# Four plain pairs instead of two ahead of the seven-product pairs, all sums off GpSimd, the last two pairs side by side

## The chip, the cores and the metric

The kernel runs on one core of a Trainium2 chip. The metric is device time in microseconds (us), the median of some runs. TensorE is called PE (its weight loads PEld), VectorE DVE, ScalarE ACT, GpSimd POOL and SyncE SP, as in the profile.

## The reference

Causal attention over 2 batches, 12 heads, 448 positions and 64 features per head, followed by two residual blocks on x of shape 2 x 448 x 768. The weights are 768 x 3072 and 3072 x 768.

```python
x = attention(q, k, v)
xn = (x - mean(x)) / sqrt(var(x) + 1e-6) * g_ln          # block 1
x = x + maximum(xn @ w_ch1, 0) @ w_ch2
x = x + real(fft(fft(x, axis=1), axis=2))                 # block 2
un = (x - mean(x)) / sqrt(var(x) + 1e-6)
x = x + maximum(un @ w2_ch1, 0) @ w2_ch2
```

## The kernel before, in words

x is held as tiles `x[b, j]` of 128 features x 448 positions (batch b of 2, feature tile j of 6). Every large product is made of three matmuls (`mm3`, L98 to L100): a float32 operand is split into a high part (ACT copy, L94) and a low part (a DVE subtraction, L95), and low x high, high x low and high x high are added in PSUM. So one product of a 128 x 128 weight tile with 448 columns is three matmuls.

A block's 3072 hidden features are 24 tiles m, taken as 12 pairs c of two. A **plain pair** (`ff1`) makes its 2 tiles for both batches from 6 feature tiles each: 2 x 2 x 6 x 3 = 72 matmuls. A **seven-product pair** (`ff1_pair`) uses the seven-product scheme for 2 x 2 blocks (the blocks are batches, halves of the features and the two tiles m): P1 to P7, each 3 tiles x 3 matmuls, 63 in all. It needs sums of the operands: on the x side `combine` makes S1 to S4 once a block (12 subtractions or additions, L716, on POOL; their splits are `xs`, L94 and L95), on the weight side every pair needs four subtractions of 128x384 (L225, on POOL but for the first pair of a block, which takes DVE). The second product of a pair (`ff2`: `ff2_sum`, then the addition onto x by DVE, L688) is 6 matmuls for each (b, j), 12 of them.

Weights come packed over SP's queue (`w_load`, 96 loads) and are unpacked by ACT (L173) and DVE (L176, `wf`), then split (`wsp`). `w_steps` is a generator that goes through the list `plan`; `w_tick` takes one step of it wherever it stands among the other instructions, and at most six `wsp` slots are held at a time. A scheduler then sets each engine's final order by what is ready and by place in the program; each engine executes its own list in order.

One block: `ff_lead` makes the hidden tiles 0 to 3 of batch 0, while the mean and the centred tiles of batch 1 are made. `ff_middle` makes tiles 0 to 3 of batch 1; meanwhile ACT and DVE make the squares (`sq`, L520, L524), PE sums them (`lnv`, L529), ACT takes the root (`sd`, L552), POOL spreads it on a diagonal (`sdiag`, L554) and PE turns that into rows (`rps`, L562), which ACT stores as `std` (L564). x is multiplied by `std` (L684: DVE for batch 0, POOL for batch 1) before the first addition. Then come the second products of the two plain pairs, ten seven-product pairs (each with the second products of the pair before as fills between its first three products), and at the end `ff2_last`: for the first three j of the order both last pairs in one PSUM sum (12 matmuls), for the other three the last pair alone (6), then the addition and a multiplication by 1/std (`rstd`, L690).

Between the blocks stands the Fourier step: `fold` adds and subtracts halves of x (`even`, `odd`, L804, L805, on POOL), folds them by position (L795 ACT, L796 and L798 DVE) and splits the result (`eo`); `stage1` multiplies with cosines and sines into `abps` (386 columns), `stage2` (`mixps`) adds to x, and `ln_sum` adds up the tiles for the next mean (`lnacc`, L494, POOL but for the last) which PE turns into `lnm` (L508). `FIRST_LAST` is the order in which `ff2_last` and `fold` take the tiles.

Of the kernel before, what the change touches and what calls it, by code (L numbers as in the profile page):

```python
# [43 lines left out]
PLAIN = 2  # L44
# [10 lines left out]
def fused_kernel(ctx: ExitStack, tc: tile.TileContext, aps, out):  # L55
# [87 lines left out]
    for moe in range(2):  # L143
        plan += [("w", moe, 1, m) for m in range(PLAIN * NM)]
        plan += [("w", moe, 2, u) for u in range(PLAIN * 2)]
        plan += [("pair", moe, c) for c in range(PLAIN, NCH)]
        plan += [("w", moe, 2, 2 * NCH - 2 + u) for u in range(2)]
# [41 lines left out]
    def w_whole(unit):  # L189
        f = decoded()  # L190
        yield True
        t = yield from w_slot(unit, 2 if unit[2] == 1 else 6)
        split(t[:, 0], t[:, 1], f, nc.gpsimd if unit[1:3] == (1, 1) else None)
        w_ready[unit] = t
        yield True

    def w_between(unit, u):
        _, moe, c = unit
        if c > PLAIN:
            yield from w_whole(("w", moe, 2, 2 * c - 2 + u))  # L200
        else:
            yield True
            yield True

    def w_steps():
        for unit in plan:
# [3 lines left out]
            half = COLS // 2  # L210
            f = decoded()
            b11, b21 = f[:, :half], f[:, half:]
            yield True
            t = yield from w_slot((unit, 0), 2)
            split(t[:, 0], t[:, 1], f)
            w_ready[unit, "P1"], w_ready[unit, "P2"] = (t, 0), (t, 3)
            yield True
            f2 = decoded()
            b12, b22 = f2[:, :half], f2[:, half:]
            yield True  # L220
            t = phalf.tile([P, 2, half], F32R, tag="h", name="wsh")
            split(t[:, 0], t[:, 1], b22)
            w_ready[unit, "P3"] = (t, 0)
            e = nc.vector if unit[2] == PLAIN else nc.gpsimd
            sub = lambda out, a, b: e.tensor_tensor(out=out, in0=a, in1=b, op=ALU.subtract)  # L225
            sub(b11, b12, b11)
            sub(b12, b22, b12)
            sub(b22, b22, b11)
            sub(b21, b21, b22)
            yield True  # L230
            yield from w_between(unit, 0)
            t = yield from w_slot((unit, 1), 2)
            split(t[:, 0], t[:, 1], f2)
            w_ready[unit, "P7"], w_ready[unit, "P6"] = (t, 0), (t, 3)
            yield True
            yield from w_between(unit, 1)
            t = yield from w_slot((unit, 2), 2)
            split(t[:, 0], t[:, 1], f)
            w_ready[unit, "P5"], w_ready[unit, "P4"] = (t, 0), (t, 3)
            yield True  # L240
# [244 lines left out]
    def ln_sum(b, j, src=x):  # L485
# [7 lines left out]
        e = nc.vector if src is xa or n_acc[b] == NJ else nc.gpsimd  # L493
        e.tensor_tensor(out=ln_acc[b], in0=acc, in1=src[b, j], op=ALU.add)  # L494
# [3 lines left out]
    def ln_rest(b, g):  # L498
# [51 lines left out]
        def deviation():  # L550
# [51 lines left out]
    def ff1_pair(moe, c, fills, after):  # L602
# [27 lines left out]
        def fill():  # L630
            for _ in range(after):
                if fills:
                    w_tick()
                    fills.pop(0)()

        kept("p1", product("P1", "a", True))
        w_tick()
        fill()
        kept("u2", product("P6", "a", False))
        w_tick()  # L640
        fill()
        kept("p7", product("P7", "b", True))
        w_tick()
        fill()
        o = product("P5", "a", False)
        added("p7", o, 1, m + 1)
        w_tick()
        o = product("P2", "c", True)
        added("p1", o, 0, m)
        w_tick()  # L650
        for name in ("P3", "P4") if c == NCH - 1 else ("P4", "P3"):
            if name == "P4":
                o = product("P4", "b", False)
                added("u2", o, 1, m)
            else:
                relu_split(0, m + 1, product("P3", "a", False))
            w_tick()
# [24 lines left out]
    def scale_x(j, b):  # L682
        e = nc.gpsimd if b else nc.vector
# [419 lines left out]
```

## Time and profile before

| what | us |
|---|---|
| median of 3 runs (855.33 to 860.99) | 855.5 |
| the profiled execution | 855.13 |
| its span, first to last instruction | 853.4 |
| PE busy | 819.7 |
| DVE busy | 661.2 |
| ACT busy | 415.4 |
| POOL busy | 238.1 |

Matmuls overlap in the pipeline: one lasts about 0.37 us in the trace and the next starts 0.20 us after it, so PE's time is read from starts, or from the number of matmuls in a stretch, not from the sum of durations. The attention ends at about 107 us; block 1 is from there to 455.6, the Fourier step to about 510 and block 2 to the end.

### The profile page before, as it was taken

To read this page: it belongs to the slowest core of one execution; us is meant where nothing else is said; L and a number is where in the kernel's file an instruction comes from. 1 tells how busy PE (TensorE), PEld (TensorE's weight loads), DVE (VectorE), ACT (ScalarE), POOL (GpSimd) and SP (SyncE) were. 2 spreads that over 40 slices of the span, in tenths; PEclk is the share of its full clock that TensorE was granted. 3 is DMA by queue.
4 is the path that set the end of the run, shared out by engine and by line. 5 is a ranking of instruction groups with operands and counts; after the bars stand their busy time and mean duration, and the time that the engine had idled before them with its cause. 6 is when DMAs were issued, how large, how long until landed. Compare 5 with 4: busy or idle time off the path is not lost. (4 is left out here: it accounts for less than half of the span.)

```text
span 853.4 us, 11883 instructions
## 1 busy us (share of the span) xinstructions
PE 819.7 (96%) x4484; PEld 730.6 (86%) x4484; DVE 661.2 (77%) x1097; ACT 415.4 (49%) x763; POOL 238.1 (28%) x230
## 2 busy tenths in 40 slices
PE   6999897999999999999997899799999999999997
PEld 5777686888999999999996779698999999999997
DVE  5778888999886777867679769999877786777744
ACT  6899997355444344433542335435444444344310
POOL 5433009422220222112057326632112220222002
PEclk9999999899999999999999799899999999999999
DMA  8431424135334224333463300113343333223003
GB/s 316 136 102 28 156 75 147 38 109 181 118 116 143 88 102 143 112 115 109 148 226 120 111 1 15 60 59 130 107 149 111 112 118 141 89 99 109 1 1 129
DMA packets 21433, 93.29 MB, mean 109 GB/s; under 512 B 2768, under 2 KB 4568, under 8 KB 21376
## 3 DMA queue, kind: packets, MB, share of 16 engines
q1 hardware_dynamic: 19152, 86.68, 30.0%
q0 software_dynamic: 2080, 5.62, 2.1%
q8 instruction: 35, 0.57, 0.3%
q14 instruction: 22, 0.18, 0.1%
q10 hardware_dynamic: 144, 0.23, 0.1%
HBM read 88.40 MB, written 2.75 MB: 107 GB/s over the span
## 5 line engine op out<-in xcount | busy, mean ns | idle before, releaser
L688 DVE TENSOR_TENSOR x<-x,yps 128x448 f32<-128x448 f32 x276 | 164.8, 613 | 100.5 <-PE yps L100 100.3
L98 PE MATMUL yps<-h,wsp 128*128 128x448 f32 x576 | 212.2, 369 | 0.8 <-ACT h L578 0.5
L99 PE MATMUL yps<-h,wsp 128*128 128x448 f32 x576 | 211.3, 367 | 0.1
L100 PE MATMUL yps<-h,wsp 128*128 128x448 f32 x576 | 210.7, 366 | 0.0
L225 POOL TENSOR_TENSOR wf<-wf 128x384 f32<-128x384 f32 x72 | 92.8, 1289 | 367.7 <-DVE wsp L95 329.4
L173 ACT ACTIVATE top<-wraw 128x768 f16<-128x768 bf16 x96 | 104.5, 1089 | 146.6 <-DVE wf L176 101.6
L95 DVE TENSOR_TENSOR wsp<-wf,wsp 128x768 fp32r<-128x768 f32 x112 | 109.4, 977 | 28.1 <-ACT wsp L94 27.8
L94 ACT ACTIVATE wsp<-wf 128x768 fp32r<-128x768 f32 x116 | 96.9, 836 | 55.3 <-PE yps L100 45.2
L176 DVE SCALAR_TENSOR_TENSOR wf<-wraw,top 128x768 uint32<-128x768 uint32 x96 | 112.6, 1172 | 9.7 <-ACT top L173 7.2
L98 PEld LDWEIGHTS yps<-h,wsp 128*128 128x128 f32 x576 | 108.5, 189 | 11.9 <-DVE x L688 1.4
L99 PEld LDWEIGHTS yps<-h,wsp 128*128 128x128 f32 x576 | 108.6, 188 | 10.1 <-issue 0.8
L100 PEld LDWEIGHTS yps<-h,wsp 128*128 128x128 f32 x576 | 108.5, 188 | 8.9 <-issue 0.2
L98 PE MATMUL hps<-xn,wsp 128*128 128x448 f32 x276 | 102.0, 370 | 0.0
L100 PE MATMUL hps<-xn,wsp 128*128 128x448 f32 x276 | 101.6, 368 | 0.0
L99 PE MATMUL hps<-xn,wsp 128*128 128x448 f32 x276 | 101.6, 368 | 0.0
L98 PE MATMUL hps<-xs,wsp 128*128 128x448 f32 x180 | 65.8, 366 | 0.0
L99 PE MATMUL hps<-xs,wsp 128*128 128x448 f32 x180 | 65.8, 365 | 0.0
L100 PE MATMUL hps<-xs,wsp 128*128 128x448 f32 x180 | 65.7, 365 | 0.0
L623 ACT ACTIVATE kept<-hps 128x448 f32<-128x448 f32 x60 | 32.3, 538 | 57.9 <-PE hps L100 57.9
L578 ACT ACTIVATE h<-kept 128x448 fp32r<-128x448 f32 x60 | 34.4, 574 | 49.0 <-DVE kept L627 48.9
L100 PEld LDWEIGHTS hps<-xn,wsp 128*128 128x128 f32 x276 | 52.2, 189 | 4.6 <-issue 0.4
L98 PEld LDWEIGHTS hps<-xn,wsp 128*128 128x128 f32 x276 | 52.3, 189 | 4.5 <-issue 0.4
(149 smaller groups left out, 1238.8 us busy)
## 6 DMA issues: line engine op xcount, KB each, us to landing
wraw<-in_w SPq DMA_DIRECT2D x96, 768.0 KB, 4.3
qkv<-in_qk SPq DMA_DIRECT2D x11, 448.0 KB, 3.5
qkv<-in_v SPq DMA_DIRECT2D x12, 256.0 KB, 4.7
out_t<-x SPq DMA_DIRECT2D x12, 224.0 KB, 1.9
x<-xr POOLq DMA_DIRECT2D x6, 222.2 KB, 2.9
cd<-in_cd POOLq DMA_DIRECT2D x3, 386.0 KB, 4.8
sd<-in_sd POOLq DMA_DIRECT2D x3, 386.0 KB, 8.1
cs<-in_cs POOLq DMA_DIRECT2D x2, 448.0 KB, 3.8
```

Source lines behind the costliest of these rows:

```text
L94: nc.scalar.activation(out=hi, in_=src, func=ACTF.Copy)
L95: (engine or nc.vector).tensor_tensor(out=lo, in0=src, in1=f32(hi), op=ALU.subtract)
L98: nc.tensor.matmul(out=dst, lhsT=w_lo, rhs=x_hi, start=first, stop=False, **kw)
L99: nc.tensor.matmul(out=dst, lhsT=w_hi, rhs=x_lo, start=False, stop=False, **kw)
L100: nc.tensor.matmul(out=dst, lhsT=w_hi, rhs=x_hi, start=False, stop=last, **kw)
L173: nc.scalar.activation(out=top_t.bitcast(F16)[:, 1::2], in_=raw.bitcast(BF16)[:, 4::4], func=ACTF.Copy)
L176: nc.vector.scalar_tensor_tensor(out=f.bitcast(U32), in0=raw.bitcast(U32)[:, 1::2], scalar=13, in1=top_t, op0=ALU.logical_shift_right, op1 ...
L225: sub = lambda out, a, b: e.tensor_tensor(out=out, in0=a, in1=b, op=ALU.subtract)
L578: nc.scalar.activation(out=t[:, 0], in_=src, func=ACTF.Relu)
L623: nc.scalar.activation(out=sums[name], in_=src, func=ACTF.Copy)
L688: nc.vector.tensor_tensor(out=xx, in0=xx, in1=y, op=ALU.add)
```

## The change

The number of plain pairs (`PLAIN`) goes from 2 to 4 a block, so 8 seven-product pairs are left instead of 10. `LEAD` keeps the four hidden tiles that are made ahead. The work for S1 to S4 is handed to the background list later: the sums with the second pair, the splits with the third and fourth. Everything that POOL added, subtracted or multiplied in the blocks and in the Fourier step goes to DVE, but for `sdiag`, which becomes four ACT copies a batch with a scale. What is left on POOL is attention's work and the loads of the cosines and sines. The last two pairs become one unit ("two"), whose products are taken in turns (P1, P1', P2, P2', ...), and all of `ff2_last` sums both pairs (12 matmuls for each (b, j)); the second products of pair 10 are no longer made apart.

```diff
-PLAIN = 2
+PLAIN = 4
+LEAD = 4
...
-        (engine or nc.vector).tensor_tensor(out=lo, in0=src, in1=f32(hi), op=ALU.subtract)
+        nc.vector.tensor_tensor(out=lo, in0=src, in1=f32(hi), op=ALU.subtract)
...
+        plan += [("pair", moe, c) for c in range(PLAIN, NCH - 2)]
+        plan += [("w", moe, 2, 2 * NCH - 6 + u) for u in range(2)] + [("two", moe, NCH - 2)]
+        plan += [("w", moe, 2, 2 * NCH - 4 + u) for u in range(4)]
...
-            e = nc.vector if unit[2] == PLAIN else nc.gpsimd
-            sub = lambda out, a, b: e.tensor_tensor(out=out, in0=a, in1=b, op=ALU.subtract)
+        sub = lambda out, a, b: nc.vector.tensor_tensor(out=out, in0=a, in1=b, op=ALU.subtract)
+        sub(b11, b12, b11)
+        sub(b12, b22, b12)
+        yield True
+        sub(b22, b22, b11)
+        sub(b21, b21, b22)
...
-        e = nc.vector if src is xa or n_acc[b] == NJ else nc.gpsimd
-        e.tensor_tensor(out=ln_acc[b], in0=acc, in1=src[b, j], op=ALU.add)
+        nc.vector.tensor_tensor(out=ln_acc[b], in0=acc, in1=src[b, j], op=ALU.add)
...
-            nc.gpsimd.tensor_tensor(
-                out=diag.rearrange("p (i t) -> p i t", i=4), in0=ident[:Q4, :Q4].unsqueeze(1).to_broadcast([Q4, 4, Q4]),
-                in1=d.unsqueeze(2).to_broadcast([Q4, 4, Q4]), op=ALU.mult,
-            )
+            for i in range(4):
+                nc.scalar.activation(
+                    out=diag[:, i * Q4 : (i + 1) * Q4], in_=ident[:Q4, :Q4], func=ACTF.Copy, scale=d[:, i : i + 1]
+                )
...
+        if len(cs) == 1:
+            for name, n in ((1, 4), (6, 4), (7, 4), (5, 0), (2, 0), (4, 0), (3, 0)):
+                run(name, n)
+        else:
+            for name, n in ((1, 4), (2, 4), (6, 0), (7, 0), (5, 0), (3, 0), (4, 0)):
+                run(name, n)
...
-        e = nc.gpsimd if b else nc.vector
-        e.tensor_tensor(out=x[b, j], in0=x[b, j], in1=std[b], op=ALU.mult)
+        nc.vector.tensor_tensor(out=x[b, j], in0=x[b, j], in1=std[b], op=ALU.mult)
...
+    def ff2_last(moe, j, b):
+        ff2_add(j, b, ff2_sum(moe, [NCH - 2, NCH - 1], j, b))
+        nc.vector.tensor_tensor(out=x[b, j], in0=x[b, j], in1=rstd[b], op=ALU.mult)
...
-            pool = lambda out, a, b, op: nc.gpsimd.tensor_tensor(out=out, in0=a, in1=b, op=op)
+            of = lambda out, a, b, op: nc.vector.tensor_tensor(out=out, in0=a, in1=b, op=op)
...
+        later_work = {1: makes, 2: splits[:HJ * 2], 3: splits[HJ * 2 :]}
         for c in range(PLAIN):
+            bg.extend(later_work.get(c, []))
+            if NM * c >= LEAD:
+                for m in range(NM * c, NM * c + NM):
+                    for b in range(B):
+                        w_tick(2)
+                        ff1(moe, m, b)
...
-        for c in range(PLAIN, NCH):
-            if c in (PLAIN + 1, PLAIN + 2):
-                invert(c - PLAIN - 1)
-            ff1_pair(moe, c, fills, 2 if c == NCH - 1 else 4)
+        for cs in [[c] for c in range(PLAIN, NCH - 2)] + [[NCH - 2, NCH - 1]]:
+            if cs[0] - PLAIN in (1, 2):
+                invert(cs[0] - PLAIN - 1)
+            ff1_pairs(moe, cs, fills)
...
-        nc.gpsimd.tensor_tensor(out=even, in0=x[b, j], in1=x[b, HJ + j], op=ALU.add)
-        nc.gpsimd.tensor_tensor(out=odd, in0=x[b, j], in1=x[b, HJ + j], op=ALU.subtract)
+        nc.vector.tensor_tensor(out=even, in0=x[b, j], in1=x[b, HJ + j], op=ALU.add)
+        nc.vector.tensor_tensor(out=odd, in0=x[b, j], in1=x[b, HJ + j], op=ALU.subtract)
```

The first place is the normalisation of block 1. POOL's list before, after the attention (`xc` are the x-side sums, `wf<-wf` the weight-side ones):

```order
L716 TENSOR_TENSOR xc<-xc 128x448 x12
L554 TENSOR_TENSOR sdiag<-ident,sd 112x448 x2
L684 TENSOR_TENSOR x<-x,std 128x448 x6
L225 TENSOR_TENSOR wf<-wf 128x384 x36
L95 TENSOR_TENSOR wsp<-wf,wsp 128x768 x2
```

And ACT's list now, at the same place in the program:

```order
L567 ACT_TABLE_LOAD
L567 ACTIVATE sd<-lnv,eps_t 112x4 x2
L570 ACTIVATE sdiag<-ident,sd 112x112 x8
L593 ACTIVATE h<-hps 128x448
L95 ACTIVATE wsp<-wf 128x768
L177 ACTIVATE top<-wraw 128x768
L579 ACTIVATE std<-rps 128x448 x2
```

The diagonal stood behind twelve sums in POOL's list; it now stands right behind the root, on the engine that makes the root. POOL's list ends with the attention, but for the loads.

The second place is the end of block 1 on DVE: the fourth and fifth of the six folds. Before:

```order
L796 TENSOR_TENSOR fold<-even 128x223
L798 TENSOR_TENSOR fold<-odd 128x223
L688 TENSOR_TENSOR x<-x,yps 128x448
L796 TENSOR_TENSOR fold<-even 128x223
L95 TENSOR_TENSOR eo<-fold,eo 128x448
L798 TENSOR_TENSOR fold<-odd 128x223
L690 TENSOR_TENSOR x<-x,rstd 128x448
L95 TENSOR_TENSOR wsp<-wf,wsp 128x768
L95 TENSOR_TENSOR eo<-fold,eo 128x448
```

Now, on DVE, from the split of the fourth fold to the split of the fifth:

```order
L713 TENSOR_TENSOR x<-x,yps 128x448 x2
L96 TENSOR_TENSOR eo<-fold,eo 128x448
L720 TENSOR_TENSOR x<-x,rstd 128x448 x2
L830 TENSOR_TENSOR even<-x 128x448
L831 TENSOR_TENSOR odd<-x 128x448
L822 TENSOR_TENSOR fold<-even 128x223
L824 TENSOR_TENSOR fold<-odd 128x223
L713 TENSOR_TENSOR x<-x,yps 128x448
L96 TENSOR_TENSOR wsp<-wf,wsp 128x768
L96 TENSOR_TENSOR eo<-fold,eo 128x448
```

`even` and `odd` have come into DVE's list, directly ahead of the folds that read them; the folds no longer wait for another engine, and the last of them stand nearer to the additions that end the block.

## Rows read from the trace of the kernel before

**Rows 1.** Part 1 of the page: busy time, share, instructions.

```profile
PE 819.7 (96%) x4484; PEld 730.6 (86%) x4484; DVE 661.2 (77%) x1097; ACT 415.4 (49%) x763; POOL 238.1 (28%) x230
```

**Rows 2.** Stretches: length; PE, PEld, DVE, ACT, POOL busy; clock, DMA share, GB/s.

```profile
142.75:154.10 11.35, 6.00 (x13) 3.45 (x12) 9.64 (x11) 3.96 (x6) 8.62 (x7) 0.70 0.41 139
154.10:200.00 45.90, 45.17 (x216) 39.89 (x215) 45.90 (x64) 20.15 (x31) 11.61 (x10) 1.00 0.21 69
200.00:455.60 255.60, 255.60 (x1263) 236.89 (x1263) 193.02 (x274) 114.53 (x165) 59.65 (x49) 1.00 0.40 133
455.60:482.00 26.40, 18.89 (x65) 15.21 (x64) 23.64 (x33) 7.56 (x14) 12.44 (x11) 0.74 0.30 96
...
506.40:509.50 3.10, 1.44 (x6) 0.68 (x5) 0.62 (x1) 0.01 (x1) 1.25 (x2) 1.00 0.00 0
...
534.00:543.60 9.60, 5.12 (x20) 4.43 (x19) 8.40 (x8) 3.06 (x6) 8.05 (x6) 0.64 0.29 104
543.60:600.00 56.40, 56.23 (x271) 50.34 (x270) 51.48 (x73) 26.25 (x40) 18.99 (x14) 1.00 0.25 85
```

**Rows 3.** PE's waits by what ended them: sum, times, longest.

```profile
PE abps L98 <- DVE eo L95: 7.5, 3, 2.8
...
PE rps L562 <- POOL sdiag L554: 5.3, 1, 5.3
...
PE lnv L529 <- ACT sd L552: 4.5, 1, 4.5
...
PE lnm L508 <- DVE lnacc L494: 1.9, 2, 1.7
```

**Rows 4.** Timeline of POOL, 133 to 160 us: start, length, instruction.

```profile
132.83 14.37 POOL L716 TENSOR_TENSOR xc<-xc 128x448 f32<-128x448 f32 x9
147.17 2.85 POOL L554 TENSOR_TENSOR sdiag<-ident,sd 112x448 f32<-112x448 f32 x2
```

**Rows 5.** Timeline of PE: steps at either clock, two small kinds.

```profile
462.46 0.53 PE L98 MATMUL abps<-sd,eo 128*112 128x386 f32 x1
462.78 0.53 PE L99 MATMUL abps<-sd,eo 128*112 128x386 f32 x1
...
465.24 0.34 PE L99 MATMUL abps<-sd,eo 128*111 128x386 f32 x1
465.42 0.33 PE L100 MATMUL abps<-sd,eo 128*111 128x386 f32 x1
...
135.30 1.64 PE L529 MATMUL lnv<-ones,sq 128*112 128x1 f32 x16
...
546.01 0.92 PE L562 MATMUL rps<-sdiag,ones 112*128 112x448 f32 x2
```

**Rows 6.** Timeline of POOL and ACT ahead of 534 us.

```profile
518.93 20.38 POOL L716 TENSOR_TENSOR xc<-xc 128x448 f32<-128x448 f32 x12 [11.21 <-ACT sq L520]
...
531.09 1.08 ACT L173 ACTIVATE top<-wraw 128x768 f16<-128x768 bf16 x1 [5.33 <-DVE wf L176]
```

**Rows 7.** DVE: a form, one instruction, two lines' minimum, median, maximum.

```profile
L176 DVE SCALAR_TENSOR_TENSOR wf<-wraw,top 128x768 uint32<-128x768 uint32 x96 | 112.6, 1172 | 9.7 <-ACT top L173 7.2
...
299.66 0.95 DVE L176 SCALAR_TENSOR_TENSOR wf<-wraw,top 128x768 uint32<-128x768 uint32 x1
...
L225 DVE TENSOR_TENSOR wf<-wf x8: 550/1078/1500, 143.9 to 544.9; 128x384 f32<-128x384 f32 x8
...
L690 DVE TENSOR_TENSOR x<-x,rstd x18: 604/624/1555, 437.7 to 849.8; 128x448 f32<-128x448 f32 x18
```

**Rows 8.** Timeline of DVE: three additions, and the last split `eo`.

```profile
308.84 1.67 DVE L688 TENSOR_TENSOR x<-x,yps 128x448 f32<-128x448 f32 x3
...
474.81 0.61 DVE L95 TENSOR_TENSOR eo<-fold,eo 128x448 fp32r<-128x448 f32 x1
```

**Rows 9.** ACT by form, an instruction of 128x128; SP's weight loads.

```profile
L378 ACT ACTIVATE pexp<-sps,stat 128x128 f32<-128x128 f32 x24 | 8.8, 367 | 7.4 <-DVE stat L366 6.7 <-DVE stat L389 0.6
...
wraw<-in_w SPq DMA_DIRECT2D x96, 768.0 KB, 4.3
```

More of the change, by code (lines that the diff above doesn't have):

```diff
@@ L91, in f32, with split @@
         return ap.bitcast(F32)
-    def split(hi, lo, src, engine=None):
+    def split(hi, lo, src):
         nc.scalar.activation(out=hi, in_=src, func=ACTF.Copy)
-        (engine or nc.vector).tensor_tensor(out=lo, in0=src, in1=f32(hi), op=ALU.subtract)
+        nc.vector.tensor_tensor(out=lo, in0=src, in1=f32(hi), op=ALU.subtract)
     def mm3(dst, w_hi, w_lo, x_hi, x_lo, first, last, **kw):
@@ L143, in fused_kernel @@
     for moe in range(2):
[L144 to L147, printed above, removed]
+        plan += [("w", moe, 1, m) for m in range(LEAD)]
+        plan += [("w", moe, 2, u) for u in range(LEAD // NM * 2)]
+        for c in range(LEAD // NM, PLAIN):
+            plan += [("w", moe, 1, NM * c + m) for m in range(NM)] + [("w", moe, 2, 2 * c + u) for u in range(2)]
+        plan += [("pair", moe, c) for c in range(PLAIN, NCH - 2)]
+        plan += [("w", moe, 2, 2 * NCH - 6 + u) for u in range(2)] + [("two", moe, NCH - 2)]
+        plan += [("w", moe, 2, 2 * NCH - 4 + u) for u in range(4)]
     for kind, moe, *at in plan:
@@ L151, in fused_kernel @@
         else:
-            raw_list += [(moe, 1, NM * at[0] + m) for m in range(NM)]
-            if at[0] > PLAIN:
+            raw_list += [(moe, 1, NM * at[0] + m) for m in range(NM if kind == "pair" else 2 * NM)]
+            if kind == "pair" and at[0] > PLAIN:
                 raw_list += [(moe, 2, 2 * at[0] - 2 + u) for u in range(2)]
@@ L209, in w_steps @@
                 continue
[L210 to L223, printed above, removed]
-            e = nc.vector if unit[2] == PLAIN else nc.gpsimd
-            sub = lambda out, a, b: e.tensor_tensor(out=out, in0=a, in1=b, op=ALU.subtract)
[L226 to L240, printed above, removed]
+            kind, moe, c = unit
+            units = [("pair", moe, c + i) for i in range(1 if kind == "pair" else 2)]
+            fs = []
+            for u in units:
+                fs.append((yield from w_firsts(u)))
+            between = kind == "pair" and c > PLAIN
+            if between:
+                yield from w_whole(("w", moe, 2, 2 * c - 2))
+            for u, (_, f2) in zip(units, fs):
+                yield from w_second(u, f2)
+            if between:
+                yield from w_whole(("w", moe, 2, 2 * c - 1))
+            for u, (f, _) in zip(units, fs):
+                yield from w_third(u, f)
     w_work = w_steps()
@@ L628, in added, with p1, p6, p7 @@
             relu_split(b, m, t)
[L630 to L657, printed above, removed]
+        def p1():
+            kept("p1", product("P1", "a", True))
+        def p6():
+            kept("u2", product("P6", "a", False))
+        def p7():
+            kept("p7", product("P7", "b", True))
+        def p5():
+            added("p7", product("P5", "a", False), 1, m + 1)
+        def p2():
+            added("p1", product("P2", "c", True), 0, m)
+        def p4():
+            added("u2", product("P4", "b", False), 1, m)
+        def p3():
+            relu_split(0, m + 1, product("P3", "a", False))
+        return p1, p2, p3, p4, p5, p6, p7
+    def ff1_pairs(moe, cs, fills):
+        steps = [pair_steps(moe, c) for c in cs]
+        def run(name, n=0):
+            for i, s in enumerate(steps):
+                s[name - 1]()
+                w_tick()
+                for _ in range(n):
+                    if fills:
+                        w_tick()
+                        fills.pop(0)()
+        if len(cs) == 1:
[4 more added lines that the diff above has]
+                run(name, n)
     def js(moe, c):
-        last = W2_ORDER if moe == 0 else list(range(NJ))
-        return last if c == NCH - 1 else last[HJ:] + last[:HJ] if c == NCH - 2 else list(range(NJ))
+        return W2_ORDER if moe == 0 and c >= NCH - 2 else list(range(NJ))
     def ff2_sum(moe, cs, j, b):
@@ L741, in ff_middle @@
         bg.extend(squares)
-        for m in range(PLAIN * NM):
+        for m in range(LEAD):
             w_tick(2)
-            if m == PLAIN * NM - 1:
+            if m == LEAD - 1:
                 while bg:
@@ L763, in ff_middle @@
                         f()
-                    for j2 in range(NJ):
-                        scale_x(j2, 1)
                 if c == 0 and n < 2:
@@ L974, in fused_kernel @@
             for j, b in FIRST_LAST:
[L975 removed]
+                ff2_last(0, j, b)
                 if (j, b) == FIRST_LAST[7]:
```

83 lines of the change are left out of this document (47 added, 36 removed).

## The prediction

> **What bounds the kernel now.** Part 1 of the page comes first: PE is busy 819.7 of 853.4 us, and no other engine comes near [rows 1]. So the question for every stretch is whether PE is fed, and at which clock. The table of stretches answers it [rows 2]. From 200 to 455.6 us PE starts 1263 matmuls in 255.6 us, one every 0.2024 us, with no gap and a clock of 1.00; the second half of block 2 is the same. There only the number of matmuls counts. The other stretches hold the losses, and the list of PE's waits names three large ones: 5.3 us for POOL's `sdiag`, 4.5 for ACT's `sd`, 7.5 in three pieces for DVE's `eo` [rows 3]. Each is followed by a stretch at half clock: the mean clock is 0.70, 0.64 and 0.74 in their stretches [rows 2], which is a part at 1.2 instead of 2.4 GHz. What each stretch loses is its length less the work in it at full clock:
>
> - 142.75 to 154.10: 11.35 us, of which eight matmuls of 448 columns (8 x 0.2024 = 1.6) and two `rps` of 0.92 [rows 5] are work. Lost: 7.9.
> - 534.0 to 543.6: 9.60 us, with ten matmuls (2.0) and half of the sixteen `lnv` that take 1.64 together (0.8) [rows 5]. Lost: 6.8.
> - 455.6 to 482: 26.40 us, 7.5 idle. A clock of 0.74 is 13.7 us at the lower level (0.26 x 26.4 / 0.5). There a 386-column matmul starts every 0.32 us instead of 0.18 [rows 5], so 0.14 of 0.32, 44%, is lost, between 2.7 us (if all idle time lay in it) and 6.0. I take 5, so 12.5 in all.
> - 154.1 to 200: 216 matmuls are 43.7 of 45.9 us, 2.2 lost; DVE is busy in all 45.90. 543.6 to 600: 267 matmuls and two `rps` are 55.9 of 56.4, 0.5 lost. Together 2.7.
> - 506.4 to 509.5: 1.7 idle, for the row sum `lnacc` [rows 2, 3].
>
> **The change, part by part.** *More plain pairs.* A plain pair has 72 matmuls where a seven-product pair has 63. Four pairs change over in the two blocks: 36 more, in the stretches where PE is full. 36 x 0.2024 = **+7.3 us**, with nothing beside them.
>
> *The diagonal on ACT, the sums off POOL.* In block 1 the twelve `xc` sums held POOL to 147.2 us, and `sdiag` could only start then [rows 4], though PE had summed the squares by 136.9 (135.30 + 1.64 [rows 5]). Now the diagonals are eight copies behind the root on ACT. Such a copy isn't in the trace; a 128x128 instruction of ACT takes 0.37 [rows 9], so 3.0 us for all, and 5.9 if they took twice as long. PE has a product of 18 matmuls (3.7 us) and two of 6 (2.4) between `lnv` and `rps`: 6.1 us to cover them. Queued behind them on ACT are the relu of tile 3, needed only by the second pair, 14.6 us later, and one weight split. Both ends lie under the cover, so I take the whole **-7.9**; if ACT came to the root late, up to 3 us would come back.
>
> In block 2 PE waited for `sd`, and ACT stood in its own list behind an unpacking that waited 5.3 us for DVE's `wf` [rows 6]. That DVE was late while POOL ran twelve sums in a row for 20.4 us [rows 6]. A `wf` takes 0.95 us alone and 1.17 on the mean; subtractions of one form range from 0.55 to 1.5 us, a multiplication from 0.60 to 1.56 [rows 7]: the long ones lie beside work of POOL. The twelve sums now cost DVE 12 x 0.62 [rows 7] = 7.4 us itself, but part of them are listed after the additions of the first pair, and the two splits and four subtractions of the first seven-product pair leave this stretch. I take the whole **-6.8**; bounds -6.8 and 0.
>
> *The end of block 1.* Before, PE finished at 455.6 and DVE's last `eo` only at 474.81 + 0.61 = 475.4 [rows 8], 20 us later, since the last six second products had only 6 matmuls each and POOL's sums lay in the chain of every fold. Now all twelve have 12: 144 x 0.2024 = 29.1 us, and as many matmuls fewer before it (no work is added, twelve DVE additions in all go). The first wait is for the fifth fold's `eo`. PE reaches it after 29.1 us and 23 matmuls of the first stage at 0.18, at 33.3 us from the start of this end phase. DVE has until then 12 additions, 11 multiplications and 10 `even` and `odd`, at 0.56 each when in a row (1.67 for three [rows 8]) 18.4 us; 12 folds of half that length, 3.3 (6.7 if they took as long); 5 splits and 2 small ones, 3.3; five weight steps of 0.95, 4.8. That is 29.8 to 33.5 us, from 2.4 us on when the first sum is there: 32.2 to 35.9, so PE waits between 0 and 2.6 us. No long gap is left that the clock would fall after. Of 12.5 us I keep 2 as lost: **-10.5**; bounds -12.5 and 0.
>
> *The saturated stretches.* The x-side sums and splits get four plain pairs to lie beside, 58 us more of PE's work in a block, and the seven-product pairs start later. Of 2.7 us I keep 0.7: **-2.0**; bounds -2.7 and a price given below.
>
> The Trainium skill speaks against taking work from POOL here: its page Perfetto Trace Analysis, section Optimizing Scalar/DVE Operations, says that offloading may make sense if DVE is saturated, even to GpSimd. It adds that the two share an SBUF read port, so that moving work between them might not help. By the first sentence the move back costs what the second rival below says; the rows on `wf` side with the second.
>
> *DVE in the seven-product pairs.* Four subtractions of 0.55 [rows 7] come into DVE's list in each of 16 pairs, 2.2 us. Against that stands what POOL's cost DVE there (`wf`: 0.22 on the mean, four a pair, 0.9). DVE was idle 62.6 of 255.6 us [rows 2]; with 135 matmuls a pair (27.3 us) that is 6.7 a pair. I cost it at nothing; behind the subtractions stand the additions that free PSUM banks, of which there are seven.
>
> *What I cost at nothing besides.* `lnacc` on DVE: five additions of 0.62 stand where four of POOL's and one of DVE's stood, behind additions onto x that are late anyway; between -1.7 and +0.5, taken as 0. The last stage of block 2: 12 matmuls (2.4 us) for every 1.2 us of DVE. SP's loads: 96 as before, 4.3 us each [rows 9] for one in about 7; the order alone changes.
>
> Sum: 7.3 - 7.9 - 6.8 - 10.5 - 2.0 = -19.9. The profiled execution took 855.13, 1.73 more than its span of 853.4 and 0.4 less than the median; 853.4 - 19.9 + 1.7 = 835.2, and I say **835.5 us**, 2.3% faster.
>
> **Rivals.** *The end of block 1 stays bound by DVE.* For it: the same folds, and twelve sums more on the engine that was late. Against: the sum above. Without the term of 10.5 the time is 853.4 + 7.3 - 16.7 + 1.7 = 845.7.
>
> *The saturated stretches get worse.* DVE had not an idle microsecond from 154.1 to 200 [rows 2]. In each block twelve sums and the six multiplications of batch 1 by `std` come to it, 18 x 0.62 = 11.2 us. If they all land where PE already waits for DVE, PE waits 22.3 us more, and the 2.0 are not gained: 853.4 + 7.3 - 25.2 + 22.3 + 1.7 = 859.5. Against: part of that 45.90 is work stretched by POOL, and the seven-product work has left.
>
> *The seven-product pairs become bound by DVE.* If the four subtractions delay the split weights of each pair by their whole length, PE waits 16 x 2.2 = 35.2 us in stretches that have no gap today: 835.2 + 35.2 = 870.4, slower. It decides from 19.9 / 16 = 1.2 us a pair on. Against: 6.7 idle us of DVE a pair.
>
> *The waits are only renamed.* The diagonal waits for ACT's list instead of POOL's, and `sd` stays late: the terms 7.9 and 6.8 fall away, and 835.2 + 14.7 = 849.9.
>
> **How the numbers follow.** A measurement of this kernel tells about 1%, 8.6 us, from no change: faster is below 846.9. The forecast has 0.74, with a range of its own from 830 (all of the losses gone, `lnacc` too) to 842; the end of block 1 bound 0.07, the renamed waits 0.05, the saturated stretches 0.07, the pairs bound 0.07. The first two cases lie below 846.9: faster 0.81. The renamed waits and the saturated stretches are within 1%: 0.12. The pairs are slower: 0.07. The range 829 to 847 holds the forecast and the first rival, a little over 8 in 10, and leaves the rest out.
>
> **What would show it.** Right: in `hps`, 1008 matmuls from `xn` and 576 from `xs`, where there were 828 and 720; no row of PE waiting for `sdiag` or `sd`; PE's waits for `eo` under 3 us in all; the clock at 1.00 from block 1 to the end; `wf` near 0.95 on the mean; the wait for `lnm` unchanged; DVE's busy time close to 661, since what it gains in work it saves in stretched instructions. Wrong: gaps of PE inside the seven-product pairs that end with `wsp` or a DVE addition; a low clock after 455 us; PE waiting for DVE between 145 and 180 us.

## The result and the profile after

The changed kernel takes **833.2 us** (median of 4 runs, 832.4 to 833.5); the kernel before, on the same chip, 858.3 (4 runs, 855.3 to 866.1). The ratio is 0.969, 95% interval 0.962 to 0.976: faster by 3.1%. The forecast was 835.5, range 829 to 847. The profiled execution took 833.47 us with a span of 831.4.

Part 1 of the page after, against [rows 1]:

```profile
PE 818.6 (98%) x4520; PEld 734.3 (88%) x4520; DVE 654.1 (79%) x1187; ACT 410.3 (49%) x759; POOL 42.2 (5%) x88
```

There are 36 matmuls more, DVE has 90 instructions more and is *less* busy, and POOL has lost 196 us. The list of PE's waits after, whole:

```profile
PE sps L365 <- DVE ks L334: 5.1, 1, 5.1
PE invps L424 <- ACT divrow L418: 1.3, 1, 1.3
PE tps L439 <- ACT pexp L394: 1.0, 2, 0.6
PE sps L365 <- DVE qs L96: 0.6, 1, 0.6
PE avps L458 <- DVE xr L484: 0.3, 1, 0.3
```

All five lie in attention. Of [rows 3] nothing is left: no `sdiag`, no `sd`, no `eo`, and no `lnm` either. The table of stretches after, for those of [rows 2] (length; busy time of PE, PEld, DVE, ACT, POOL; clock, DMA share, GB/s):

```profile
142.75:154.10 11.35, 11.35 (x54) 9.88 (x53) 10.49 (x18) 7.66 (x17) 0.00 (x0) 1.00 0.31 114
154.10:200.00 45.90, 45.90 (x229) 42.54 (x228) 39.97 (x64) 20.41 (x28) 0.00 (x0) 1.00 0.48 156
...
453.70:480.10 26.40, 26.40 (x133) 22.39 (x132) 21.21 (x41) 10.27 (x18) 0.00 (x0) 1.00 0.35 120
480.10:513.40 33.30, 33.30 (x164) 29.83 (x163) 31.06 (x60) 18.01 (x35) 0.00 (x0) 1.00 0.06 19
513.40:600.00 86.60, 86.60 (x433) 79.53 (x433) 69.99 (x113) 36.37 (x59) 0.00 (x0) 1.00 0.31 103
```

The clock is 1.00 in every one and PE is never idle. The first 26.4 us of the Fourier step hold 133 matmuls, where the kernel before started 65. DVE's unpackings, for [rows 7]:

```profile
L180 DVE SCALAR_TENSOR_TENSOR wf<-wraw,top 128x768 uint32<-128x768 uint32 x96 | 91.7, 955 | 9.8 <-ACT top L177 9.1
```

Without POOL beside it an unpacking takes 0.955 us where it took 1.172 on the mean, and the same 96 cost 91.7 us instead of 112.6.

**Where the time went.** The last matmul of attention, the first of the Fourier step (`abps`), its last (`mixps`) and the last of all cut the trace in pieces; a row gives the first and the last start of a line. (Attention's last matmul before starts at 109.3 us, not at the 107 of the section on the time before.) The kernel before, then after:

```profile
L442 PE MATMUL avps<-pT,qkv x480: 222/272/473, 16.0 to 109.3; 128*64 128x128 f32 x96, 128*64 128x64 f32 x64
...
L98 PE MATMUL abps<-cd,eo x12: 335/386/667, 455.6 to 489.6; 128*113 128x386 f32 x6, 128*112 128x386 f32 x6
...
L100 PE MATMUL yps<-h,wsp x576: 362/365/575, 140.9 to 848.7; 128*128 128x448 f32 x192
...
L100 PE MATMUL mixps<-sn,ab x12: 360/368/368, 482.1 to 503.1; 112*128 112x448 f32 x6, 111*128 111x448 f32 x6
```

```profile
L458 PE MATMUL avps<-pT,qkv x480: 222/272/476, 19.5 to 114.2; 128*64 128x128 f32 x96, 128*64 128x64 f32 x64
...
L99 PE MATMUL abps<-cd,eo x12: 334/342/432, 453.7 to 474.2; 128*113 128x386 f32 x6, 128*112 128x386 f32 x6
...
L101 PE MATMUL yps<-h,wsp x576: 358/365/369, 145.8 to 826.7; 128*128 128x448 f32 x192
...
L101 PE MATMUL mixps<-sn,ab x12: 360/363/367, 466.7 to 487.0; 112*128 112x448 f32 x6, 111*128 111x448 f32 x6
```

| piece | before | after | difference | forecast |
|---|---|---|---|---|
| to the end of attention | 109.3 | 114.2 | +4.9 | 0 |
| block 1 | 346.3 | 339.5 | -6.8 | -5.9 |
| Fourier step | 47.5 | 33.3 | -14.2 | -10.5 |
| block 2 | 345.6 | 339.7 | -5.9 | -3.5 |

(The forecast gives each block 18 x 0.2024 = 3.65 us of added matmuls, and of the 2.0 for the saturated stretches 1.6 to block 1 and 0.4 to block 2.) The blocks and the Fourier step gave 26.9 us instead of 19.9; attention, whose code is the same, took 4.9 back. That the time was forecast within 2.3 us is luck: two errors nearly cancel. In medians of the same chip the gain is 858.3 - 833.2 = 25.1 us, where the forecast had 20; it started from a median of 855.5.

### The profile page after: what moved, and what is told of

Its sections match the earlier page's. It is cut to its first block, busy times and chain, and to the rows that moved or that the text cites. A ratio compares the mean times of both kernels' runs of the same rounds, so it can differ in the third digit from the quotient of the medians.

```text
span 831.4 us, 11846 instructions
## 1 busy us (share of the span) xinstructions
PE 818.6 (98%) x4520; PEld 734.3 (88%) x4520; DVE 654.1 (79%) x1187; ACT 410.3 (49%) x759; POOL 42.2 (5%) x88
## 4 chain that ended last, share of the span: by engine, by line
PE 97%; ACT 1%; DVE 1%; DMA 0%; issue 0%; DVEq 0%
PE yps L99 14%; PE yps L100 14%; PE yps L101 14%; PE hps L99 13%; PE hps L101 13%; PE hps L100 13%; PE tps L439 3%; PE sps L365 3%; PE avps L458 3%; PE mixps L99 1%; PE mixps L100 1%; PE mixps L101 1%; PE invps L424 1%; PE abps L99 1%; ACT pexp L394 1%; PE abps L100 1%
## 5 line engine op out<-in xcount | busy, mean ns | idle before, releaser
L713 DVE TENSOR_TENSOR x<-x,yps 128x448 f32<-128x448 f32 x264 | 159.7, 619 | 67.4 <-PE yps L101 65.5
L177 ACT ACTIVATE top<-wraw 128x768 f16<-128x768 bf16 x96 | 104.5, 1088 | 110.1 <-DVE wf L180 81.6
L95 ACT ACTIVATE wsp<-wf 128x768 fp32r<-128x768 f32 x112 | 94.2, 842 | 110.7 <-PE yps L101 88.6
L96 DVE TENSOR_TENSOR wsp<-wf,wsp 128x768 fp32r<-128x768 f32 x112 | 107.0, 956 | 26.6 <-ACT wsp L95 25.6
L99 PE MATMUL hps<-xn,wsp 128*128 128x448 f32 x336 | 123.2, 367 | 0.0
L101 PE MATMUL hps<-xn,wsp 128*128 128x448 f32 x336 | 123.2, 367 | 0.0
L100 PE MATMUL hps<-xn,wsp 128*128 128x448 f32 x336 | 123.0, 366 | 0.0
L180 DVE SCALAR_TENSOR_TENSOR wf<-wraw,top 128x768 uint32<-128x768 uint32 x96 | 91.7, 955 | 9.8 <-ACT top L177 9.1
L101 PEld LDWEIGHTS hps<-xn,wsp 128*128 128x128 f32 x336 | 63.1, 188 | 5.4 <-issue 0.4
L99 PEld LDWEIGHTS hps<-xn,wsp 128*128 128x128 f32 x336 | 63.1, 188 | 5.4 <-issue 0.4
L100 PEld LDWEIGHTS hps<-xn,wsp 128*128 128x128 f32 x336 | 63.1, 188 | 5.1 <-issue 0.2
L101 PE MATMUL hps<-xs,wsp 128*128 128x448 f32 x144 | 52.6, 366 | 0.0
L99 PE MATMUL hps<-xs,wsp 128*128 128x448 f32 x144 | 52.6, 368 | 0.0
L100 PE MATMUL hps<-xs,wsp 128*128 128x448 f32 x144 | 52.6, 365 | 0.0
L594 DVE SCALAR_TENSOR_TENSOR h<-hps,h 128x448 fp32r<-128x448 f32 x48 | 29.7, 622 | 21.9 <-ACT h L593 21.5
L394 ACT ACTIVATE pexp<-sps,stat 128x128 f32<-128x128 f32 (+3 forms) x84 | 41.4, 508 | 7.5 <-DVE stat L382 7.4
```

The lines of the kernel that those rows point to most:

```text
L96: nc.vector.tensor_tensor(out=lo, in0=src, in1=f32(hi), op=ALU.subtract)
L99: nc.tensor.matmul(out=dst, lhsT=w_lo, rhs=x_hi, start=first, stop=False, **kw)
L100: nc.tensor.matmul(out=dst, lhsT=w_hi, rhs=x_lo, start=False, stop=False, **kw)
L101: nc.tensor.matmul(out=dst, lhsT=w_hi, rhs=x_hi, start=False, stop=last, **kw)
L177: nc.scalar.activation(out=top_t.bitcast(F16)[:, 1::2], in_=raw.bitcast(BF16)[:, 4::4], func=ACTF.Copy)
L180: nc.vector.scalar_tensor_tensor(out=f.bitcast(U32), in0=raw.bitcast(U32)[:, 1::2], scalar=13, in1=top_t, op0=ALU.logical_shift_right, op1 ...
```

## The experiments

The twelve runs were made on four chips, each beside runs of the kernel before on its chip. "Blocks" below is the time from the last matmul of attention to the last of all, from such rows as above; it is 739.4 before and 712.5 after. Each run has one trace. Where two versions ran on different chips, their ratios to the kernel before are the fairer comparison.

**The diagonal alone.** The kernel before with

```diff
-            nc.gpsimd.tensor_tensor(
...
+            for i in range(4):
+                nc.scalar.activation(
+                    out=diag[:, i * Q4 : (i + 1) * Q4], in_=ident[:Q4, :Q4], func=ACTF.Copy, scale=d[:, i : i + 1]
+                )
```

> The kernel before with one edit: the diagonal as four ACT copies a batch instead of one POOL multiplication. Theory: the term of 7.9 us alone. PE's wait of 5.3 us for sdiag and the low clock behind it (147 to 154 us) go; block 2, where PE waited for ACT's root and not for the diagonal, and the Fourier step stay. 855.5 - 7.9 = 847.6. Rival, the waits are only renamed: rps then waits for another instruction in the same place and the time stays within 3 us of the kernel before. Second rival: it helps block 2 as well, since the two diagonals there were POOL's too, up to 841.

Measured 860.0 (853.7 to 864.6) against 857.5 (853.8 to 866.1), ratio 1.001 (0.997 to 1.005). PE's waits:

```profile
PE abps L98 <- DVE eo L95: 5.0, 2, 2.8
PE yps L98 <- DVE x L688: 5.0, 3, 2.4
```

The wait for `sdiag` is gone, and 5.0 us for additions onto x stand in its place (159 to 179 us). The wait was renamed: block 1 takes 345.3 us in this trace, 1.0 less than before, and the times show no difference. (The trace is of the fastest of ten executions, 853.7 us. Its blocks is 735.6; of the 3.8 us less, 2.8 lie in the Fourier step, 44.7 us against 47.5, which this edit doesn't touch.) The timeline shows DVE beside POOL's work there:

```profile
155.45 1.56 DVE L684 TENSOR_TENSOR x<-x,std 128x448 f32<-128x448 f32 x1
156.94 1.48 DVE L225 TENSOR_TENSOR wf<-wf 128x384 f32<-128x384 f32 x1
158.34 0.61 DVE L688 TENSOR_TENSOR x<-x,yps 128x448 f32<-128x448 f32 x1
158.87 0.55 DVE L225 TENSOR_TENSOR wf<-wf 128x384 f32<-128x384 f32 x1
```

The multiplication by `std` takes 1.56 us instead of 0.61, the subtraction 1.48 instead of 0.55, until POOL pauses. Not every instruction is lengthened. In the kernel before, two lines of DVE (minimum, median, maximum in ns):

```profile
L688 DVE TENSOR_TENSOR x<-x,yps x276: 600/612/623, 152.0 to 849.1; 128x448 f32<-128x448 f32 x138
...
L176 DVE SCALAR_TENSOR_TENSOR wf<-wraw,top x96: 940/952/1912, 82.6 to 798.2; 128x768 uint32<-128x768 uint32 x96
```

The additions onto x, whose second input lies in PSUM, take 0.60 to 0.62 us with POOL at work or not; the unpackings, with both inputs in SBUF (the tiles' own memory), take up to twice their 0.95. Why is not shown here.

**The engine move without the plain pairs and without the new ending.** Two plain pairs (`PLAIN = 2`, `later_work = {0: makes, 1: splits}`), the last two pairs one after the other, 6 matmuls for three of the last tiles; everything off POOL.

> The change without its two other parts: two plain pairs and the old ending, but all of POOL's sums on DVE and the diagonal on ACT. With two plain pairs and the new ending 837.3 was measured, and the ending made no difference with four pairs. Theory: 837 within 2, the same PE waits of about 7 us for additions onto x in the first second products (DVE has the twelve x-side sums there), and no wait over 3 us for eo. So the engine move is worth some 20 us by itself. Rival, with two pairs the old ending falls behind again: waits for eo of 5 us and more, 843 to 848.

Measured 838.1 (836.1 to 840.2), ratio 0.977 (0.971 to 0.982); blocks 719.6.

```profile
PE yps L99 <- DVE x L714: 6.2, 7, 1.6
...
PE abps L99 <- DVE eo L96: 1.2, 1, 1.2
```

As expected: by the traces the engine move alone is worth 739.4 - 719.6 = 19.8 of the 26.9 us, and what it leaves is mostly DVE late in the first second products. The reverse, four pairs with every sum still on POOL, was not run.

**Two plain pairs, with the new ending.**

> The changed kernel with two plain pairs, as the kernel before has, everything else of the change kept. Theory: 36 matmuls fewer than the changed kernel, 7.3 us, 825.9 at best; but the sums (12 x 0.62 = 7.4 us) and the splits (12 x 0.6 = 7.3 us) on DVE then fall into the first two pairs' second products beside the six multiplications and twelve additions, as in the kernel before, where 154 to 200 us had DVE busy without a pause. I expect 2 to 6 us of PE waits there in the two blocks, so 828 to 832, with waits of PE for wsp, xs or a DVE addition between 150 and 200 us. Rival B, the number of pairs is only a count: no such waits, 826. Rival A, four pairs are needed: over 833, with waits over 7 us.

Measured 837.3 (836.3 to 842.1), ratio 0.976 (0.972 to 0.981).

```profile
PE yps L99 <- DVE x L713: 7.3, 7, 1.6
...
PE hps L99 <- DVE x L713: 0.4, 1, 0.4
```

Blocks is 724.1, of which 6.4 are the longer step of PE told further down (1600 matmuls), so 717.7. By its waits that is rival A: 7.7 us, more than my 2 to 6, and low clock behind two of them. The time says less, since without the longer step the profiled execution would have taken 833.2. The third and fourth pair pay for their 7.3 us of matmuls and save some 5 besides; that four are needed does not follow (see three pairs).

**The old ending alone.** The changed kernel with

```diff
-        for cs in [[c] for c in range(PLAIN, NCH - 2)] + [[NCH - 2, NCH - 1]]:
+        for cs in [[c] for c in range(PLAIN, NCH)]:
...
-        ff2_add(j, b, ff2_sum(moe, [NCH - 2, NCH - 1], j, b))
+        early = js(moe, NCH - 1).index(j) < HJ
+        ff2_add(j, b, ff2_sum(moe, [NCH - 2, NCH - 1] if early else [NCH - 1], j, b))
```

> The changed kernel with the ending of the kernel before: the last two pairs one after the other, and the second product of the last pair alone (6 matmuls) for three of the six tiles of x. All sums stay on DVE. Theory: the twelve second products that end block 1 shrink from 144 matmuls (29.1 us) to 108 (21.9), DVE has twelve additions more, and PE comes to the fifth fold 7.3 us earlier than DVE has it: by the sum of the prediction (32.2 to 35.9 us of DVE against 33.3 of PE) waits of 6 to 10 us for eo, and a low clock behind one of them; 833.2 + 6 to 12 = 839 to 845. Rival, the move of even, odd and the multiplications off POOL was what removed these waits: within 2 us of 833.

Measured 832.6 (831.4 to 834.0), ratio 0.970 (0.965 to 0.975): the rival. One wait for `eo` is left, 1.2 us, with no low clock behind it:

```profile
PE abps L99 <- DVE eo L96: 1.2, 1, 1.2
...
PE hps L99 <- ACT xn L550: 0.9, 1, 0.9
```

Blocks is 715.9, 3.4 more, 0.7 of it the longer step; so the side-by-side ending is worth 2 to 3 us in the traces and nothing that the times could tell.

**The folds' sums on POOL.** The changed kernel with `even` and `odd` issued by `nc.gpsimd`.

> The changed kernel with even and odd of the Fourier step back on POOL (12 sums of 1.4 us in the kernel before, against 0.56 to 0.62 on DVE). The kernel with the old ending lost only 1.2 us for eo, so the ending was not what removed the 12.5 us. Theory: it was POOL in the chain of each fold (2.8 us for the two sums, and stretched DVE work beside them). With the new ending and POOL in the chain PE then waits for eo again, 2 to 5 us, with 1.5 to 3 us of low clock behind it: 833.2 + 3.5 to 8 = 836.5 to 841. Rival, the other work that left DVE's neighbourhood (multiplications, row sums) was enough, or either edit alone suffices: no wait for eo, 832 to 834.

Measured 841.6 (839.8 to 842.1), ratio 0.980 (0.976 to 0.985): 8.4 us above the changed kernel, and a little above the theory's 836.5 to 841.

```profile
PE abps L99 <- DVE eo L96: 6.1, 1, 6.1
```

```profile
450.00:486.50 36.50, 30.36 (x136) 25.33 (x135) 25.47 (x42) 11.44 (x21) 8.39 (x6) 0.86 0.27 94
```

Twelve instructions on the other engine bring the wait, longer than the 2 to 5 us expected, and a mean clock of 0.86 back; the Fourier step takes 42.9 us, 9.6 more than in the changed kernel. The timeline shows the difference, here with POOL (first its own sum, then DVE):

```profile
455.45 1.51 POOL L831 TENSOR_TENSOR odd<-x 128x448 f32<-128x448 f32 x1
...
455.90 1.32 DVE L822 TENSOR_TENSOR fold<-even 128x223 f32<-128x223 f32 x1
457.14 0.38 DVE L824 TENSOR_TENSOR fold<-odd 128x223 f32<-128x223 f32 x1
...
461.55 1.31 DVE L822 TENSOR_TENSOR fold<-even 128x223 f32<-128x223 f32 x1 [1.02 <-POOL even L830]
```

and in the changed kernel:

```profile
454.82 0.39 DVE L822 TENSOR_TENSOR fold<-even 128x223 f32<-128x223 f32 x1
455.12 0.39 DVE L824 TENSOR_TENSOR fold<-odd 128x223 f32<-128x223 f32 x1
```

The fold of `even` runs while POOL makes `odd`, and takes 1.31 us instead of 0.39; the fold of `odd` behind it finds POOL idle and takes 0.38 (POOL's sum ends at 456.96 us, its next starts at 459.80). So POOL costs twice: its own 1.1 to 1.9 us a sum, and what lies beside it.

**The pairs' sums on POOL.** The changed kernel with the 24 x-side sums and the 64 weight-side subtractions on `nc.gpsimd`.

> The changed kernel with the 24 x-side sums and the 64 weight-side subtractions back on POOL (1.65 and 1.29 us each in the kernel before); four plain pairs, the diagonal on ACT, the folds and the ending stay. Theory: wf rises from 0.955 us back to about 1.15 on the mean and other DVE work of 128x448 beside POOL to 1.0 or more, but in the pairs DVE has 6 idle us and the x-side sums now lie beside plain pairs, so PE waits less than 2 us in all: 832 to 836. Rival, working side by side with POOL is itself the loss: PE waits for yps or hps behind a DVE addition as in the kernel before (5 us and low clock a block): 840 or more.

Measured 843.5 (837.7 to 844.4), ratio 0.982 (0.977 to 0.986), more than the theory gave. The time is the rival's (840 or more), but its waits, for a DVE addition, are not there; the wait that came is another:

```profile
PE rps L577 <- ACT std L579: 3.2, 1, 3.2
```

```profile
129.99 19.22 POOL L739 TENSOR_TENSOR xc<-xc 128x448 f32<-128x448 f32 x12 [38.90 <-ACT xc L735]
...
507.16 21.60 POOL L739 TENSOR_TENSOR xc<-xc 128x448 f32<-128x448 f32 x12 [80.68 <-ACT sq L535]
```

```profile
519.18 1.88 DVE L96 TENSOR_TENSOR wsp<-wf,wsp 128x768 fp32r<-128x768 f32 x1
521.15 1.75 DVE L180 SCALAR_TENSOR_TENSOR wf<-wraw,top 128x768 uint32<-128x768 uint32 x1
...
522.93 1.10 ACT L177 ACTIVATE top<-wraw 128x768 f16<-128x768 bf16 x1 [4.26 <-DVE wf L180]
```

In block 2 the scheduler let POOL run its twelve sums right behind the squares, from 507 to 529 us; there DVE's weight work doubles to 1.75 and 1.88 us, ACT waits for it, and `std` comes 3.2 us late, with a low clock of 3.4 us behind. In block 1 POOL ran them at the same place, from 130 to 149 us, and PE waited for nothing there; why block 2 alone suffered isn't shown. In the pairs the theory held: by the list PE waits 1.3 us there, for `h` and `kept`. Blocks is 725.5, 13 us more, and 4 of them are the longer step again (some 1000 matmuls). The Trainium skill, Perfetto Trace Analysis, section Optimizing Scalar/DVE Operations, names GpSimd as a place for work of a saturated DVE and warns that a shared SBUF port may spoil it. The trace agrees with the warning: `wf` is at 1.084 us on the mean, against 0.955 in the changed kernel.

**Two small jobs on POOL.** The changed kernel with the diagonals, and all of `lnacc` but the last, on `nc.gpsimd`.

> The changed kernel with two small jobs back on POOL: the four diagonals (1.44 us each) and the row sums lnacc, but for the last of each batch. Theory: POOL is idle there, so the diagonal costs nothing without the sums ahead of it (no PE wait for sdiag over 0.5 us): the wait of 5.3 us was POOL's list, not its speed. The row sums at 1.2 us a piece bring back a wait for lnm of up to 1.7 us behind the Fourier step. 833.2 + 0 to 2 = 833 to 835.5. Rival for lnacc: its wait before came from late additions onto x (DVE), and stays away: 833.

Measured 834.6 (832.0 to 836.1), ratio 0.972 (0.968 to 0.976).

```profile
PE lnm L524 <- DVE lnacc L510: 1.7, 1, 1.7
```

The wait for `lnm` is back at its 1.7 us, so it was POOL's row sums; there is none for `sdiag`. (Blocks is 717.6, 5.1 more; 2.7 of it are the longer step.) An idle POOL makes the diagonal in time: before, it was its place behind twelve sums that was late.

**How much DVE the pairs bear.** `for _ in range(8): sub(scr, b22, b11)` behind the four subtractions of each seven-product pair.

> The changed kernel with eight more DVE subtractions of 128x384 in each seven-product pair (behind the fourth, into a tile that nothing reads): 16 x 8 x 0.55 = 70 us more work for DVE, 4.4 us a pair. In the changed kernel DVE is idle 94.8 of 420 us in the two stretches of pairs, 6.2 us of 27.3 a pair. Theory: 4.4 fits under 6.2, and what is queued behind it (weight splits, additions that free PSUM banks) has slots ahead: less than 3 us in all, 833 to 836, DVE busy about 724. Rival, DVE's order is tight and each addition in the list delays the pair: up to 70 us more, over 850.

Measured 837.8 (836.6 to 838.8), ratio 0.976 (0.973 to 0.980); DVE's busy time 710.8.

```profile
PE hps L99 <- DVE kept L645: 3.3, 2, 3.0
PE hps L99 <- ACT kept L641: 1.3, 2, 0.6
```

DVE's busy time rose by 56.7 us, not 70 (an instruction starts up to 0.1 us before the one ahead of it ends, as the timelines above show), for twice the subtractions that the change itself put into each pair. PE waits 4.6 us for it, more than the 3 of the theory, and the time lies 1.8 us above its range (2.8 more of the 8.1 us in blocks are the longer step). So DVE doesn't bind the pairs with the four subtractions that the change gave it; with twelve it begins to.

**Three plain pairs.** `PLAIN = 3`, `later_work = {1: makes, 2: splits}`.

> The changed kernel with three plain pairs instead of four; the x-side sums lie beside the second, all their splits beside the third. Theory: from block 1 on PE is never idle, so only the number of matmuls counts. One pair less in each block is made plain, 2 x 9 = 18 matmuls fewer, 18 x 0.2024 = 3.6 us: 833.2 - 3.6 = 829.6, as long as DVE keeps up in the 29 us a block that are left for the splits; PE's count falls from 4520 to 4502. Rival A, four pairs are needed: the splits come late, PE waits for xs or wsp in the pairs behind, and the time is 833 or more. Rival B, the engine move alone does the work and the number of pairs is only a count: 829.6 as well, but then the next run with two gives 826.

Measured 831.4 (830.7 to 833.7), ratio 0.969 (0.965 to 0.973). Rival A falls: PE waits for nothing behind attention. But blocks is 715.5, not 708.9, though every matmul was fed. The table of stretches shows it, here and then in the next run, which is the same program on another chip:

```profile
205.00:380.00 175.00, 175.00 (x848) 158.92 (x848) 138.36 (x210) 78.57 (x110) 0.00 (x0) 1.00 0.34 118
390.00:450.00 60.00, 60.00 (x298) 55.60 (x297) 50.62 (x86) 27.51 (x44) 5.88 (x11) 1.00 0.53 186
```

```profile
205.00:380.00 175.00, 175.00 (x865) 162.09 (x864) 141.02 (x216) 80.41 (x115) 0.00 (x0) 1.00 0.35 119
```

848 matmuls in 175 us without a gap, at a granted clock of 1.00, against 865: a step of 206.7 ns instead of 202.7. It begins in the first seven-product pair of each block and lasts 864 matmuls; 2 x 864 x 4.0 ns = 6.9 us.

> The three-pair kernel once more, unchanged. Theory: the longer step belongs to the order of the program, so this trace shows 206.7 ns again, from the first seven-product pair on and over 864 matmuls in each block, and the time is 831.4 within 1. Rival, it comes and goes by chance: another stretch or none, a time between 824 and 831. What may differ from run to run is the start: clock records at 1.00 have begun between 10.5 and 21.7 us in the traces so far, and the end of attention between 109.1 and 114.2.

Measured 827.1 (824.3 to 829.4), ratio 0.964 (0.960 to 0.969), blocks 708.6 (the trace is of the fastest execution, 824.3), and no stretch of the longer step. So the order of the program alone doesn't decide it: the theory of this run falls.

**Fills for the first seven-product pair.** Three plain pairs and

```diff
+                if c == PLAIN - 1 and n >= 8:
+                    fills.append(lambda c=c, j=j, b=b: ff2(moe, c, j, b))
+                    continue
```

> The three-pair kernel with four second products of the last plain pair kept as fills for the first three products of the first seven-product pair. In the trace of the three-pair kernel PE was never idle in the pairs and the clock 1.00, and still 864 matmuls in each block started every 206.7 ns instead of 202.7: 1728 x 4.0 ns = 6.9 us. Both times this began behind one matmul that came 0.09 us late, in the first seven-product pair, where the second product writes to the PSUM bank that ACT is still copying (kept) and no other work lies between. Theory: that late matmul throws PE into the longer step. With the fills there is none, the step stays at 202.7 and the time is 831.4 - 6.9 = 824.5. Rival A, the step has another cause (the addresses or the loads of this stretch): it is 206.7 here too, 831. Rival B, it comes and goes by chance: the runs spread between 824 and 831.

Measured 827.2 (825.8 to 828.2), ratio 0.964 (0.960 to 0.968), blocks 708.4, no longer step. Its time was to be 824.5, but on the same chip the kernel without fills has no longer step either: the run doesn't tell.

**The changed kernel once more.**

> The changed kernel once more, unchanged. Two things of its first trace were not in the sum: attention ended 4.8 us later than in the kernel before (114.2 against 109.3 us), though its code is the same, and PE's clock rose to 1.00 only at 21.7 us instead of 10.7. Theory: this start varies from run to run; other traces ended attention at 109.1 to 112.6. I expect an end of attention between 109 and 114 and from there to the last matmul 712.5 us as in the first trace (826.7 - 114.2), within 0.5 if no stretch of 206.7 ns comes: 828.5 to 833.5, and against the three-pair kernel (827.1 on another chip) 3.6 us more on the mean. Rival: the change itself makes attention's end later, then it is 114 again and 833.

Measured 833.8 (831.5 to 836.0), ratio 0.973 (0.9715 to 0.9745). Attention's end and the end of all:

```profile
L458 PE MATMUL avps<-pT,qkv x480: 222/272/476, 19.2 to 111.4; 128*64 128x128 f32 x96, 128*64 128x64 f32 x64
...
L101 PE MATMUL yps<-h,wsp x576: 358/368/369, 143.0 to 829.3; 128*128 128x448 f32 x192
```

Attention ended 2.8 us earlier than in the first trace, and the blocks took 717.9: 5.4 us more, and the longer step is there, over some 1340 matmuls (x 4.0 ns = 5.4). Against the three-pair kernel the median is 6.7 us more, where 3.6 was expected; the longer step stands in this trace and not in that one.

## Why the prediction was right, and where it was not

*More plain pairs, +7.3.* The cost is right: from three pairs to four, 18 matmuls more in all, blocks grows by 712.5 - 708.6 = 3.9 us, 3.65 by the count. What I put under it is not. I priced the pairs as cost only, with 2.0 us of relief; against two pairs (717.7 without the longer step) they buy back 717.7 - 712.5 + 7.3 = 12.5 us of waits and low clock. But three pairs do that as well as four, so half of the 7.3 is paid for nothing. The second rival, the saturated stretches, shows there in small: with two pairs PE waits 6 to 8 us for DVE, not 22.3; with four, not at all.

*The diagonal and the sums off POOL, -7.9 and -6.8.* Block 1 gave 6.8 with 3.65 of new matmuls, so 10.4 of loss went, against 9.5 forecast. The step that I drew is only part of the cause: with the diagonal on ACT alone, 5 us of waits come up 10 to 30 us later and the time stays. The rival "the waits are only renamed" was true of that edit by itself. What removes them is that DVE isn't late any more, and neither part does that alone: with POOL silent but two pairs, 6 to 8 us of waits are left; with four pairs and the pairs' sums on POOL, block 1 lost some 1 us beside the longer step, but block 2 had its 3.2 for `std`. Block 2 gave 5.9, with the new matmuls 9.6 of loss; 1.7 of that is `lnacc`, told below, which leaves 7.9 against 7.2 forecast. The chain that I read there (twelve sums on POOL, a late `wf`, a late ACT) is the one that came back with the pairs' sums on POOL.

*The end of block 1, -10.5 of 12.5.* The loss was 14.2, beyond my bound of 12.5, and all of it is gone: 7.5 idle and 6.7 besides, by the low clock for the most part, where I took 5 from a range of 2.7 to 6.0; the low clock lay over more work than I took. Some of the 14.2 belongs to that execution, for the trace with the diagonal alone has the same Fourier code and takes 2.8 us less. And of the two causes that I named, the ending counts for 2 to 3 us once the sums are on DVE (the Fourier step is 36.2 with the old ending, 33.3 with the new), POOL in the chain of the folds for most of the rest: taking it back costs 9.6 us of that step, 8.4 in the medians. (DVE's upper figure in my sum adds up to 33.2, not 33.5, so 35.6 and a wait of at most 2.3; nothing hangs on it.)

*`lnacc` taken as 0.* Wrong: the 1.7 us went and come back with the sums on POOL. I held the additions onto x for the late ones; a POOL addition of 1.2 us in a chain of five was.

*DVE in the seven-product pairs at nothing, busy time near 661.* Right: 654.1, `wf` at 0.955, and eight more subtractions a pair bring waits of 4.6 us.

*Attention.* Not in the sum, and it took 4.9 us. In the fourteen traces of this case, all with the same attention, its end lies between 109.1 and 114.2 us, so it is no effect of the change; what goes with it is told under the start, at the end.

## What to carry to other kernels

An engine that seems free may not be: here sums on POOL lengthened DVE instructions beside them that read SBUF alone, so look at the minimum and maximum of one form before offloading, and count both. A wait for one engine can hide a later wait for another; take it away alone before crediting it. Three plain pairs are enough here: at 831.4 and 827.1 us (ratios 0.969 and 0.964; 827.2 with the fills) that version has the lowest times that were run, and the count of matmuls gives it 3.65 us over the changed kernel (ratios 0.969 and 0.973), which the times alone hardly tell.

## What was not expected of the hardware

*Two steps at one clock.* With PE fed and the clock at 1.00, matmuls of 448 columns start either every 202.7 ns (steps of 199 to 207 mixed) or every 206.7 (206 or 207 each), for hundreds in a row, and nothing between. The same program had no such stretch in a trace on one chip and 6.9 us of it on another; the changed kernel had 0.15 us in its first trace and 5.4 in its second. In three traces (three pairs, the changed kernel's second, the small jobs) it begins and ends at the same places of both blocks, within a few matmuls; in others it stands in one block alone, or in both over different lengths (two pairs). What decides it wasn't found.

*The start.* From 10.8 to 18.8 us the changed kernel started 34 matmuls, the kernel before 68:

```profile
10.80:18.80 8.00, 7.62 (x34) 5.51 (x34) 4.50 (x20) 5.75 (x19) 6.02 (x11) 1.00 1.03 411
```

```profile
10.80:18.80 8.00, 7.47 (x68) 5.42 (x66) 5.32 (x22) 7.41 (x27) 6.03 (x11) 1.00 1.03 410
```

PE is as busy in both, so each matmul lasts twice as long, though the table gives 1.00; the first record of the clock stands at 21.7 us in the one and at 10.7 in the other. So the 1.00 of this row may be no more than the want of a record. The three-pair kernel with fills has a record at half clock there, from 13.2 to 20.1 us, and 41 matmuls:

```profile
10.80:18.80 8.00, 7.36 (x41) 5.43 (x43) 5.30 (x22) 7.03 (x25) 6.01 (x11) 0.65 1.03 408
```

The end of attention goes with this start in all fourteen traces, before and changed alike: 109.1 to 110.1 us where the first record, at 1.00, stands at 10.5 to 10.8 us, 111.2 to 111.8 where it stands at 18.6 to 19.5, 112.6 in the trace with fills (1.00 again from 20.1) and 114.2 where it stands at 21.7. What makes it late in some executions is open.
